# Reordering two start-up transposes on TensorE and moving satisfied waits of ScalarE to a later stage

## The chip, the cores and the metric

One core of one Trainium2 chip. The metric is device time in microseconds (us) of one execution. In the profile of the kernel before, that time is the span (first to last instruction) plus 1.2 to 1.3 us. "Granted clock" is the share of TensorE's full clock that the chip let it run at. All executions below count as undisturbed ones ("fast").

## The reference, cut to what matters

Two branches share the input x (2048 tokens of 640): linear attention with a softmax feature map, and a SwiGLU FFN of width 1728. A sigmoid gate, one number per token, mixes them.

```python
g = sigmoid((x * gate_w).sum(-1, keepdims=True))
a = attention(x, wqkv, w_phi, wo)      # phi(q) (phi(k)^T v) / (phi(q) . sum phi(k)), then @ wo
b = (silu(x @ w_gate) * (x @ w_up)) @ w_down
out = g * a + (1 - g) * b
```

## The kernel before

Every operation is one letter in a list that is worked through in order, and every engine gets its instructions in that order. `H` is a pair of dummy matmuls, `G` transposes the gate row, `X t` transposes token tile t, `U t.c` is part c (of five) of v tile t, `V` a whole v tile, `F b.k` an FFN item, `M` premultiplies K's weights by the feature map's, `K` a key tile, `a` 88 waits on ScalarE, `N` the end of the kv sums. The other letters don't matter here.

```python
ORDER = """
H0 H1 a H2 H3 H4 H5 H6 H7 H8 H12 G X0 H9 H10 U0.0 X1 H11 U1.0 U0.1 U1.1 X2 U2.0 U0.2 U1.2 U2.1
X3 U2.2 U0.3 U1.3 U2.3 U0.4 U1.4 U2.4 V3 Y F0.1 M1 i3 M0 F0.0 M2 V4 M3 M4 K0 K1 ...   # cut
"""
def act_waits():                                  # 'a'
    for _ in range(NWAIT):                        # 88
        act.wait_ge(tr.sem["pe"], 1)              # true since the first dummy pair
def xpose(t):                                     # 'X'
    pr = next_pair()
    for c0, c1 in (((0, 1), (1, 5)) if t < 3 else ((0, 5),)):
        o = bankbf(2 * pr + (c0 > 0), 640)
        transposes([(o[:, c * P:(c + 1) * P], xs[:, t, c * P:(c + 1) * P]) for c in range(c0, c1)])
        copy("dve", xT[:, t, c0:c1, :].rearrange("p c k -> p (c k)"), o[:, c0 * P:c1 * P])
def v_out(t, pr):                                 # after a v tile's last part
    ...                                           # cut
    copy("act", o, i)                             # the first ScalarE computation of the program
    copy("act", svec[:, t:t + 1], bank(2 * pr + 1, 320, 321))
def kv_end():                                     # 'N'
    for _ in range(NPEW):                         # 24
        pe.wait_ge(tr.sem["pe"], 1)
    ...                                           # cut
```

The softmax here doesn't subtract the row's maximum and nothing guards it: scores larger than these inputs give would overflow.

Of the kernel before, what the change touches and what calls it, by code (L numbers as in the profile page):

```python
# [15 lines left out]
NPE = 4  # L16
NV = 6
NWARM = 2
NWAIT = 88
NPEW = 24  # L20
FP = 120 * NCH
FK = FP + 8
ACTF = mybir.ActivationFunctionType
# [12 lines left out]
"""  # L36

ORDER = """
H0 H1 a H2 H3 H4 H5 H6 H7 H8 H12 G X0 H9 H10 U0.0 X1 H11 U1.0 U0.1 U1.1 X2 U2.0 U0.2 U1.2 U2.1
X3 U2.2 U0.3 U1.3 U2.3 U0.4 U1.4 U2.4 V3 Y F0.1 M1 i3 M0 F0.0 M2 V4 M3 M4 K0 K1 I S0 V6 V5 S1 P0  # L40
K3 K2 P1 E0 V9 K4 E1 S3 V7 P3 K5 S2 V8 V10 S4 P2 P4 E2 R0 E3 K6 S5 P5 S6 i4 E4 V14 K7 K8 P6 V15 S7
R2 E5 K9 S8 P7 R1 E6 K10 S9 V12 P8 E7 P9 K11 S10 P10 F0.2 R3 F1.2 E8 E9 K12 E10 S11 S12 K14 S14
# [11 lines left out]
class _Tracker:  # L54
# [90 lines left out]
    def run(self, eng, fn, reads=(), writes=(), dma=False):  # L145
        rkeys = list(dict.fromkeys(k for a in reads for k in self.keys_of(a)))
        wkeys = list(dict.fromkeys(k for a in writes for k in self.keys_of(a)))
        need = {}

        def req(ev, raw):  # L150
            if ev is None:
                return
            s, v = ev
            if s == eng and not dma and (eng == "pe" or not raw):
                return
            if v > need.get(s, 0):
                need[s] = v

        for k in rkeys:
            for kk in self._conflicts(k):  # L160
                req(self.lastw[kk], True)
                if k[0] == "psum":
                    for s, v in self.readers[kk].items():
                        req((s, v), False)
        for k in wkeys:
            for kk in self._conflicts(k):
                req(self.lastw[kk], True)
                for s, v in self.readers[kk].items():
                    req((s, v), False)
        self._wait(eng, need)  # L170
        ins = fn()
        if dma:
            sn = "d%d" % self.ndma
            self.ndma += 1
            self._add_sem(sn)
            inc = 16
        else:
            sn, inc = eng, 1
        ins.then_inc(self.sem[sn], inc)
        self.cnt[sn] += inc  # L180
        v = self.cnt[sn]
        snap = dict(self.known[eng])
        if not dma:
            snap[sn] = max(snap.get(sn, 0), v)
        self.evknow.setdefault(sn, {})[v] = snap
        ev = (sn, v)
        for k in wkeys:
            self.lastw[k] = ev
            self.readers[k] = {}
        for k in rkeys:  # L190
            r = self.readers[k]
            if r.get(sn, 0) < v:
                r[sn] = v
        return ev


def _build(nc, A_x, A_wqkv, A_w_phi, A_wo, B_x, B_w_gate, B_w_up, B_w_down, gate_w, out):
    tr = _Tracker(nc)
    pe, act, dve, pool, sp = nc.tensor, nc.scalar, nc.vector, nc.gpsimd, nc.sync
# [76 lines left out]
    def bank(b, c0, c1, r0=0, r1=P):  # L276
        return ps[r0:r1, b * 512 + c0:b * 512 + c1]
# [9 lines left out]
    def mm(pairs):  # L287
        reads, writes = [], []
        for p in pairs:
            reads += [p[1], p[2]]  # L290
            writes.append(p[0])

        def fn():
            last = None
            for o, l, r, st, sp_, sk in pairs:
                last = pe.matmul(o, lhsT=l, rhs=r, start=st, stop=sp_, skip_group_check=sk)  # L296
            return last
        return run("pe", fn, list({id(a): a for a in reads}.values()), writes)

    def group(o, lr):  # L300
        n = len(lr)
        return [(o, l, r, i == 0, i == n - 1, False) for i, (l, r) in enumerate(lr)]
# [9 lines left out]
    def actop(o, i, func, scale=1.0):  # L312
        rd = [i] + ([scale] if isinstance(scale, bass.AP) else [])
        return run("act", lambda: act.activation(o, i, func, scale=scale), rd, [o])  # L314
# [7 lines left out]
    def tt(e, o, a, b, op):  # L322
        eo = tr.eng[e]
        return run(e, lambda: eo.tensor_tensor(o, a, b, op), [a, b], [o])  # L324

    def stt(o, a, s, b, op0, op1):
        rd = [a, b] + ([s] if isinstance(s, bass.AP) else [])
        return run("dve", lambda: dve.scalar_tensor_tensor(  # L328
            out=o, in0=a, scalar=s, in1=b, op0=op0, op1=op1), rd, [o])
# [45 lines left out]
    def load_ffn(c0, c1):  # L375
        dma("sp", wg[:, :, c0:c1], B_w_gate[:, c0:c1].rearrange("(c p) j -> p c j", p=P))
        dma("sp", wu[:, :, c0:c1], B_w_up[:, c0:c1].rearrange("(c p) j -> p c j", p=P))
# [19 lines left out]
    H0 = [0, 6, 12, 19, 25]  # L397
    H1 = [7, 13, 20, 26, 32]
# [24 lines left out]
            memset("pool", ph[:, :, :], 0.0)  # L423
            memset("pool", zh[:, NCH:P], 0.0)

    def act_waits():
        for _ in range(NWAIT):
            act.wait_ge(tr.sem["pe"], 1)

    for i in range(3):  # L430
        fills(i)

# [21 lines left out]
    def next_pair():  # L454
        return used([r for r in ring["lru"] if r < ring["n"] and r not in held][0])
# [224 lines left out]
    def fitem(bt, k):  # L680
        buf = bt % 2
        pr = next_pair()
        xr = [xT[:, 4 * bt:4 * bt + 4, c, :] for c in range(5)]
        u = us[:, nus[0] % 3, :]
        nus[0] += 1
        if k < 13:
            g, up = bank(2 * pr, 0, 512), bank(2 * pr + 1, 0, 512)
            h = hT[:, buf, k, :]
            mm(group(g, [(wg[:, c, P * k:P * k + P], xr[c]) for c in range(5)]))
            mm(group(up, [(wu[:, c, P * k:P * k + P], xr[c]) for c in range(5)]))  # L690
        else:
            mm(group(bank(2 * pr, 0, 512), [(wt[:, c, :], xr[c]) for c in range(5)]))
            g, up = bank(2 * pr, 0, 512, 0, 64), bank(2 * pr, 0, 512, 64, P)
            h, u = hT[0:64, buf, k, :], u[0:64]
        actop(h, g, ACTF.Tanh, 0.5)
        actop(u, up, ACTF.Copy)
        stt(h, h, 1.0, g, ALU.add, ALU.mult)
        tt("pool", h, h, u, ALU.mult)
# [43 lines left out]
    def kv_end():  # L742
        for _ in range(NPEW):
            pe.wait_ge(tr.sem["pe"], 1)
        kv_finish()
        ring["n"] = 4
# [3 lines left out]
        "M": lambda m: premult(1, m), "R": lambda m: premult(0, m),  # L750
        "K": ktile, "S": knorm, "P": kmul, "p": lambda t: kmul(t, "dve"), "E": kvtile, "x": load_x, "t": load_xt, "w": load_wv, "h": load_phi, "k": lambda m: load_wt(1, m), "q": lambda m: load_wt(0, m),
        "f": lambda i: load_ffn(FCUT[i], FCUT[i + 1]), "L": load_late_weights, "T": tail_weights, "J": gates,
        "Y": w_blocks, "a": lambda: act_waits(), "I": kv_begin, "N": kv_end, "Z": z_row,
        "Q": qtile, "A": qsum, "B": qden, "C": qscale, "c": qmul,
        "F": fitem, "O": oitem, "D": ditem,
    }
    for w in LOADS.split() + ORDER.split():
# [4 lines left out]
def bass_gated_mix__linear_kernel_hedgehog__swiglu_ffn__prompt_kernel(  # L762
    nc: bass.Bass,
    A_x: bass.AP,
    A_wqkv: bass.AP,
    A_w_phi: bass.AP,
    A_wo: bass.AP,
    B_x: bass.AP,
    B_w_gate: bass.AP,
    B_w_up: bass.AP,  # L770
    B_w_down: bass.AP,
    gate_w: bass.AP,
    out: bass.AP,
):
    _build(nc, A_x, A_wqkv, A_w_phi, A_wo, B_x, B_w_gate, B_w_up, B_w_down, gate_w, out)
# [28 lines left out]
```

## Time and profile before

| | before, first profile | before, second profile |
|---|---|---|
| time of that execution, us | 289.45 | 289.25 |
| span, us | 288.2 | 288.0 |
| first matmul of the first FFN item, us | 12.10 | 11.89 |
| last matmul's start, us | 286.11 | 285.90 |
| from the one to the other, us | 274.02 | 274.02 |

The second profile was taken after the prediction. The median before was 290.37 us of 3 runs when the prediction was written, and 290.72 of 6 in the comparison that followed. The views that the argument rests on are in the prediction and are not shown again.

### The profile page before, as it was taken

How to read it: one execution, taken by the hardware profiler on the slowest of the kernel's cores; microseconds unless marked ns; L12 is line 12 of the kernel's file. 1: busy time of each engine (PE TensorE's matmuls, PEld its weight loads, DVE VectorE, ACT ScalarE, POOL GpSimd, SP SyncE). 2: the span in 40 equal slices, each digit the busy share in tenths (PEclk: the TensorE clock that was granted, in tenths of full speed). 3: DMA queues.
4: the chain of work that ended last, by engine and by line, in shares of the span. 5: the costliest groups of instructions: out<-in, count | busy, mean ns of one | idle time of the engine just before them, and what ended most of it. 6: DMA issues, size and time to landing. Idle time of an engine off the chain costs nothing.

```text
span 288.2 us, 4961 instructions
## 1 busy us (share of the span) xinstructions
PE 284.9 (99%) x1975; PEld 174.8 (61%) x1975; DVE 163.5 (57%) x243; ACT 151.6 (53%) x252; POOL 159.8 (55%) x125
## 2 busy tenths in 40 slices
PE   8999999999999999999999999999999999999997
PEld 6567777575644445557775556675554446656776
DVE  2146748577469978679991475970317899100000
ACT  0678768666685566583445753225676552234112
POOL 8286899879545789836633438350753558501000
PEclk9999999999999999999999999999999999999999
DMA  6975789000020498302292002061020006210101
GB/s 209 185 113 125 113 212 369 9 0 3 0 50 0 104 306 152 63 2 50 55 165 63 12 1 50 2 144 47 2 50 0 3 1 123 52 45 0 49 23 48
DMA packets 48944, 21.62 MB, mean 75 GB/s; under 512 B 39384, under 2 KB 48792, under 8 KB 48920
## 3 DMA queue, kind: packets, MB, share of 16 engines
q1 hardware_dynamic: 48190, 20.62, 31.5%
q10 hardware_dynamic: 730, 0.68, 0.7%
q8 instruction: 16, 0.26, 0.4%
q14 instruction: 8, 0.07, 0.1%
HBM read 9.29 MB, written 2.62 MB: 41 GB/s over the span
## 4 chain that ended last, share of the span: by engine, by line
PE 98%; ACT 1%; DVE 0%; issue 0%; ACTq 0%
PE ps L296 97%; PE ps L478 1%; PE ps L308 1%; ACT L314 0%; ACT v1r L314 0%; DVE xT L320 0%; DVE osb L730 0%; ACTq L139 0%; ACT svec L314 0%
## 5 line engine op out<-in xcount | busy, mean ns | idle before, releaser
L324 POOL TENSOR_TENSOR hT<-hT,us 128x512 bf16<-128x512 bf16 (+1 forms) x56 | 65.0, 1173 | 67.0 <-DVE hT L328 50.1
L328 DVE SCALAR_TENSOR_TENSOR hT<-hT,ps 128x512 bf16<-128x512 bf16 (+1 forms) x56 | 37.4, 683 | 69.0 <-ACT hT L314 55.3
L296 PE MATMUL ps<-xT,wg 128*128 128x512 bf16 x260 | 64.6, 379 | 0.4 <-ACT svec L314 0.4
L296 PE MATMUL ps<-xT,wu 128*128 128x512 bf16 x260 | 64.6, 379 | 0.0
L296 PE MATMUL ps<-wd,hT 128*128 128x320 bf16 (+2 forms) x462 | 63.9, 295 | 0.0
L324 POOL TENSOR_TENSOR ph<-eq,qc 128x1320 bf16<-128x1320 bf16 x16 | 42.3, 2645 | 25.6 <-DVE qc L638 20.8
L296 PEld LDWEIGHTS ps<-wd,hT 128*128 128x128 bf16 x462 | 44.5, 98 | 17.4
L296 PE MATMUL ps<-wqk,xT 128*128 128x320 bf16 x320 | 47.7, 299 | 0.0
L314 ACT ACTIVATE hT<-ps 128x512 bf16<-128x512 f32 (+2 forms) x60 | 35.8, 597 | 16.0 <-PE ps L296 15.8
L296 PEld LDWEIGHTS ps<-xT,wu 128*128 128x128 bf16 x260 | 25.5, 98 | 30.6
L314 ACT ACTIVATE us<-ps 128x512 bf16<-128x512 f32 (+1 forms) x56 | 33.5, 598 | 19.2 <-PE ps L296 18.2
L296 PEld LDWEIGHTS ps<-xT,wg 128*128 128x128 bf16 x260 | 25.0, 98 | 28.4 <-ACT oT L314 0.8
L314 ACT ACTIVATE osb<-ps,omg 128x640 bf16<-128x640 f32 (+2 forms) x17 | 12.9, 757 | 55.8 <-PE ps L296 55.8
L324 POOL TENSOR_TENSOR ekr<-ekr,krec 128x1280 bf16<-128x1280 bf16 x16 | 37.4, 2357 | 5.7 <-DVE krec L338 5.7
L296 PEld LDWEIGHTS ps<-wqk,xT 128*128 128x128 bf16 x320 | 30.5, 98 | 13.1 <-issue 0.4
L314 ACT ACTIVATE eq<-ps 128x640 bf16<-128x640 f32 x32 | 22.3, 703 | 20.8 <-POOL ph L324 10.6
L335 DVE TENSOR_REDUCE ksum<-ekr 128x64 f32<-128x1280 bf16 x16 | 23.5, 1471 | 11.7 <-ACT ekr L314 11.7
L314 ACT ACTIVATE ekr<-ps 128x640 bf16<-128x640 f32 x32 | 22.3, 703 | 8.7 <-PE ps L296 8.2
L335 DVE TENSOR_REDUCE qz<-eq 128x64 f32<-128x1280 bf16 x16 | 23.7, 1479 | 2.6 <-ACT eq L314 2.6
L296 PE MATMUL ps<-wvg,xT 128*128 128x320 bf16 (+1 forms) x160 | 24.6, 301 | 0.1
L296 PE MATMUL ps<-wog,oT 128*128 128x320 bf16 (+2 forms) x165 | 24.7, 295 | 0.0
L335 DVE TENSOR_REDUCE qw<-ez 128x64 f32<-128x1280 bf16 x16 | 23.6, 1477 | 0.0
(73 smaller groups left out, 189.8 us busy)
## 6 DMA issues: line engine op xcount, KB each, us to landing
out_dram<-osb SPq DMA_DIRECT2D x15, 160.0 KB, 1.9
wd<-in_B_w_down_dram SPq DMA_DIRECT2D x1, 2080.0 KB, 9.5
wg<-in_B_w_gate_dram SPq DMA_DIRECT2D x1, 1040.0 KB, 9.5
wu<-in_B_w_up_dram SPq DMA_DIRECT2D x1, 1040.0 KB, 10.7
wg<-in_B_w_gate_dram SPq DMA_DIRECT2D x1, 800.0 KB, 5.6
wu<-in_B_w_up_dram SPq DMA_DIRECT2D x1, 800.0 KB, 7.2
wog<-in_A_wo_dram SPq DMA_DIRECT2D x2, 375.0 KB, 7.2
wvg<-in_A_wqkv_dram SPq DMA_DIRECT2D x4, 160.0 KB, 4.0
```

The costliest lines, as they stand in the source:

```text
L296: last = pe.matmul(o, lhsT=l, rhs=r, start=st, stop=sp_, skip_group_check=sk)
L308: last = pe.transpose(o, i, ident[0:k, 0:k])
L314: return run("act", lambda: act.activation(o, i, func, scale=scale), rd, [o])
L324: return run(e, lambda: eo.tensor_tensor(o, a, b, op), [a, b], [o])
L328: return run("dve", lambda: dve.scalar_tensor_tensor(out=o, in0=a, scalar=s, in1=b, op0=op0, op1=op1), rd, [o])
L335: return run("dve", lambda: dve.tensor_reduce(o, i, AX.X, ALU.add), [i], [o])
L478: last = pe.matmul(bank(2 * pr, 0, P), lhsT=c, rhs=c, start=True, stop=True)
```

## The change

Its intent: TensorE's start-up is reordered so that copies hide behind other work, and the spare waits leave the start of ScalarE's stream, where they stood ahead of its first computation. They come back in the third FFN stage, and TensorE gets eight more waits at the end of the kv sums, so that the instruction streams stay nearly as long as they were. Two of the 26 dummy matmuls go.

```diff
-NWAIT = 88
-NPEW = 24
+NWAIT = 6
+NPEW = 32
-H0 H1 a H2 H3 H4 H5 H6 H7 H8 H12 G X0 H9 H10 U0.0 X1 H11 U1.0 U0.1 U1.1 X2 U2.0 U0.2 U1.2 U2.1
+H0 H1 H2 H3 H4 H5 H6 G H7 H8 X0 H9 H10 U0.0 X1 H11 U1.0 U0.1 X2 U1.1 U2.0 U0.2 U1.2 U2.1
-    def act_waits():
-        for _ in range(NWAIT):
-            act.wait_ge(tr.sem["pe"], 1)
@@ fitem
+        if bt == 2:
+            for _ in range(NWAIT):
+                act.wait_ge(tr.sem["pe"], 1)
         actop(h, g, ACTF.Tanh, 0.5)
```

More of the change, by code (lines that the diff above doesn't have):

```diff
@@ L752, in _build @@
         "f": lambda i: load_ffn(FCUT[i], FCUT[i + 1]), "L": load_late_weights, "T": tail_weights, "J": gates,
-        "Y": w_blocks, "a": lambda: act_waits(), "I": kv_begin, "N": kv_end, "Z": z_row,
+        "Y": w_blocks, "I": kv_begin, "N": kv_end, "Z": z_row,
         "Q": qtile, "A": qsum, "B": qden, "C": qscale, "c": qmul,
```

## The prediction

> **What bounds the kernel now.** I read the page's busy shares first, then the waits of TensorE, then the chain of work that ended last, then the timeline of the first 14 us.
>
> ```profile
> PE 284.9 (99%) x1975; PEld 174.8 (61%) x1975; DVE 163.5 (57%) x243; ACT 151.6 (53%) x252; POOL 159.8 (55%) x125
> ```
>
> TensorE is busy for 284.9 of 288.2 us and every other engine for under 60%. So the span is TensorE's work plus TensorE's holes, and a change that alters no matmul of the real work can only win or lose holes. The waits of TensorE, which list only the holes the profile calls idle, are two:
>
> ```profile
> PE ps L478 <- PEq L789: 0.8, 1, 0.8
> PE ps L296 <- ACT svec L314: 0.4, 1, 0.4
> ```
>
> The chain of work (start us, us, what) shows where the head of the kernel loses time and that nothing is lost later:
>
> ```profile
> 6.48 0.07 PE ps L308
> 6.55 0.02 issue
> 6.57 0.23 DVE xT L320
> 6.80 0.05 issue
> 6.85 1.27 PE ps L296 x8
> 8.12 0.28 PE ps L308 x5
> 8.40 1.39 PE ps L296 x10
> 9.79 0.02 issue
> 9.81 0.04 ACTq L139
> ...
> 9.95 1.28 ACT L314
> 11.24 0.01 issue
> 11.25 0.71 ACT v1r L314
> 11.95 0.07 ACT svec L314
> 12.02 0.07 issue
> 12.10 66.26 PE ps L296 x616
> 78.36 0.05 PE ps L308
> 78.41 207.92 PE ps L296 x1271
> ```
>
> From 12.10 us to 286.33 us it is matmul after matmul. A matmul's modelled end overlaps the next, so I also took the start-to-start steps of all 1975 matmul records against the usual step of their size (136 ns for 320 columns, 216 for 512, 55 for 128 once warm). After 12.1 us only eight steps are over by more than 25 ns, some 94 ns each, at the four tiles' kvsb matmuls. Before it: 0.25 us at 4.36 us (the first v part waits for weights landing at 4.22), 0.21 us at 6.85 us (x2's copy on VectorE, the 0.23 us above), and 0.56 us at 12.10 us, where the first FFN item waits until ScalarE has emptied the first v tile's banks. ScalarE is late because of this:
>
> ```profile
> 8.24 3.46 PE L296 MATMUL ps<-wvg,xT 128*128 128x320 bf16 x24
> 12.10 1.24 PE L296 MATMUL ps<-xT,wg 128*128 128x512 bf16 x5 [0.40 <-ACT svec L314]
> 9.95 1.28 ACT L314 ACT_TABLE_LOAD   x1 [9.95 <-PE ps L296]
> 11.25 0.71 ACT L314 ACTIVATE v1r<-ps 128x640 bf16<-128x640 f32 x1
> 11.85 0.17 ACT L314 ACTIVATE svec<-ps 128x1 f32<-128x1 f32 x1
> ```
>
> The table load starts only after the matmul that the first evacuation needs. In the built program waits are packed two to an instruction, and with 88 spare waits in front the real wait on TensorE (semaphore at 34) slides forward into a wait instruction ahead of the load. The spare waits themselves are done early: this view of their line gives 43 records, 3.2 to 6.4 us.
>
> ```profile
> L428 ACTq EVENT_SEMAPHORE  x43: 17/38/38, 3.2 to 6.4; - x43
> ```
>
> **What the Trainium skill says.** "ScalarE: Activation LUTs", section What ACT_TABLE_LOAD costs, gives about 1283 ns for the load itself; the trace has 1.28 us, and the new program has exactly one load too. "Perfetto Trace Analysis", section Identifying Dependency Chains, says that instructions waiting on several engines may get EventSemaphore instructions ahead of them; the 43 records for 88 waits agree. "TensorE: Matmul & The Clock Gate", Part 1, puts the rise of the clock around 4 us into activity, ±500 ns from run to run. Here matmuls of 128 columns step by 107 ns from 0.84 us and by 55 from about 5.2 us, 4.3 us in. "Runtime: NRT & Kernel Launch", section Instruction fetch mechanics, says instructions come in 16 KiB blocks; the page's instruction queue q8 has 16 packets and 0.26 MB, so TensorE's do, and its last such packet falls at 285.2 us, near the end.
>
> **The change part by part.**
>
> (1) Start-up dummies: 26 become 24, and the gate row's transpose comes after 14 instead of 20. x0 lands at 3.08 us whichever order is used, and the first v part waits for weights landing at 4.22 us. Before, x0 was transposed at 3.18. Four dummies after the gate row end near 0.84 + 18 x 0.107 + 0.11 + 0.14 = 3.0 us. The first v part stays at 4.36 us: 0.
>
> (2) x2 ahead of v part U1.1. Before: six matmuls (U1.0, U0.1, U1.1) from 5.48, x2 from 6.32, a hole, U2.0 at 6.85. After: x2 from 6.04 (landed 5.56; its second bank waits for x1's second copy, done at 5.93), its first column block finished by about 6.26, copied by 6.52, while U1.1's two matmuls fill 6.32 to 6.59. U2.0 starts at about 6.59 instead of 6.85: **0.26 us earlier**. The next limits: x3 lands at 7.56 and its matmul was at 7.96, w3 at 8.05 against 8.51. They leave 0.36 and 0.41 us after a floor of about 0.05, so the 0.26 passes.
>
> (3) No waits ahead of the table load. In the new program the load waits only for the memset of the v tiles (GpSimd, done by about 5 us), so it ends near 6.2 us; the wait for TensorE sits on the evacuation. That then runs at 9.79 - 0.26 = 9.53 us instead of 11.25 and is done near 10.3, before V3's last matmul. The **0.56 us** hole goes; its gate and up weights landed at 9.30 and 10.41. The FFN item starts at 12.10 - 0.26 - 0.56 = 11.28 us.
>
> (4) But loads do not come earlier. Setting each landing against the first matmul that waits for it, three early ones are close: premultiply M2's weights land at 16.33 for a matmul at 17.04 (0.71), M4's at 18.49 for 19.05 (0.56), the others have 1.3 us or more. A released matmul starts 0.05 us after its landing at best (x2's copy shows 0.046). So TensorE may shift 0.66 us at M2 and **0.51 us** at M4. Of the 0.26 + 0.56 = 0.82 us won, 0.31 is given back waiting for M2's and M4's weights. From there the K tiles follow M4 through the same copies, and all later stages shift together.
>
> (5) 84 waits in the third FFN stage: 6 per item, 14 items, three wait instructions each at a pace of 75 ns (two of them at 9.81 and 9.89), 0.23 us per item, 3.2 us of ScalarE. Most of them pass while ScalarE waits for TensorE anyway; the last of the three holds the real wait, so a tanh starts at most 0.1 us later after its matmul. In 154 to 222 us ScalarE is busy 36.6 of 68 us. The closest bank releases of that stage stand 0.51 us or more ahead of the matmul that needs them: 0.
>
> (6) Eight more waits on TensorE, four instructions at a pace of 0.106 us, 0.42 us. The eleven old ones run from 75.8 to 76.9 us while the queue still holds Q2's matmuls until 78.19. The margin falls from some 1.1 to 0.7 us: 0. Counted in the two programs, TensorE's instructions go from 4045 to 4046 and ScalarE's from 360 to 358: these added waits keep the streams' lengths, so the block that is fetched at the end stays where it was.
>
> Sum: 290.37 - 0.51 = **289.9 us**.
>
> **The rivals.** (a) Loads land earlier or M4's limit is not real: the full 0.82 us, 289.5. For: landings of that stage differ between executions, and the transposing loads are issued one after another on SyncE with steps from 1.26 to 3.8 us. Against: in this trace M4's slack is 0.56. (b) The head's gain is eaten wholly, because landings decide when the K stage starts, or because the clock rises half a microsecond later: 290.4. For: the skill's ±500 ns and a DMA share over 0.8 in the first 12 us. Against: no hole before M2 in the trace. (c) ScalarE's added waits turn into a TensorE hole in the third stage: from 198.6 to 204.8 us ScalarE works without a break, and three items of 0.23 us could add 0.7 us there, giving 290.6. Against: 0.5 to 0.9 us of slack, and only some of the items there are of that stage. (d) The end: a shift of the last instruction fetch against the last stores, a few tenths either way.
>
> **Range and chances.** The three timed runs before reach from 290.0 to 291.07, and the profiled one took 289.45, so the noise of a median of three (some 0.3 us) is as large as the gain. Rival (a) sets 289.5 and (c) 290.6; with the noise around them I take 289.2 to 290.8. Two per cent is 5.8 us, eleven times the gain; the whole of TensorE's holes before 12.1 us plus the end after 286.3 would not make it, and no part adds a serial cost near it. Same 0.97, faster 0.02, slower 0.01.
>
> **What would show it.** Right: the table load ends before 8 us, the wait of 0.4 us on svec is gone, U2.0 starts near 6.6 us, the FFN item near 11.3, and M2 or M4 starts within 0.1 us of its weights' landing; TensorE ends some 0.5 us earlier. (4) is wrong if the K stage starts 0.8 us earlier or not earlier at all. (5) and (6) are wrong if TensorE shows a new hole between 154 and 270 us, or near 78 us. The whole is wrong if the last matmul moves by more than 1 us.

## The result, and the profile after

The kernel after took 289.3 us in the median of 6 runs (288.35 to 289.61), the kernel before 290.72 us in the same rounds (290.0 to 291.73): ratio 0.9942, 95% interval 0.9915 to 0.997. Ratios here are the mean time of one kernel's fast runs over that of the other's of the same rounds, so not quite the ratio of the medians. By the medians the gain is 1.4 us, where the prediction had 0.5 (the 289.3 us lie at the low end of its range). Yet the profiled execution after has a span of 288.0 us, only 0.2 less than the first profile before. That contradiction is what the experiments had to settle.

The waits of TensorE in the kernel after: the one on svec is gone, and a load has come in its place.

```profile
PE ps L474 <- PEq L788: 0.8, 1, 0.8
PE ps L296 <- DMA wvg<-in_A_wqkv_dram: 0.7, 2, 0.4
```

ScalarE's timeline of the kernel after (start us, us, instruction): the table load starts at 5.01 us instead of 9.95 and is over long before the first evacuation, which begins at 10.20 instead of 11.25.

```profile
5.01 1.28 ACT L314 ACT_TABLE_LOAD   x1 [5.01 <-POOL v1r L342]
10.20 0.71 ACT L314 ACTIVATE v1r<-ps 128x640 bf16<-128x640 f32 x1 [3.91 <-PE ps L296]
```

The chain that ended last in the kernel after (start us, us, what) begins with a load. The second piece of the v weights landed at 6.37 us, against 5.38 in the first profile before. That ate most of what the closed holes had given: the first FFN item starts at 11.92 us, inside the long piece that begins at 8.79.

```profile
1.73 4.64 DMA wvg<-in_A_wqkv_dram
...
6.41 0.45 PE ps L296 x2
...
8.79 69.40 PE ps L296 x640
```

From the first matmul of the first FFN item to the last matmul of all, the kernel after takes 274.02 us, as before, to 10 ns. The same stretch was measured in all 20 traces: 274.01 or 274.02 us in 18 of them, whatever ScalarE's and TensorE's waits were, and 274.30 and 274.31 in two that come up below. **So, those two apart, everything that the change did to the span lies before that matmul**, in the head of the kernel, and the question is what that head does from one execution to the next.

### The profile page after: what moved, and what is told of

Read it like the earlier page.

```text
span 288.0 us, 4960 instructions
## 1 busy us (share of the span) xinstructions
PE 284.6 (99%) x1973; PEld 174.1 (60%) x1973; DVE 163.5 (57%) x243; ACT 151.8 (53%) x252; POOL 159.8 (55%) x125
## 4 chain that ended last, share of the span: by engine, by line
PE 97%; DMA 2%; SPq 0%; DVE 0%; issue 0%
PE ps L296 97%; DMA wvg<-in_A_wqkv_dram 2%; SPq L350 0%; PE ps L308 0%; DVE osb L729 0%
## 6 DMA issues: line engine op xcount, KB each, us to landing
wu<-in_B_w_up_dram SPq DMA_DIRECT2D x1, 1040.0 KB, 11.9
```

## The experiments

All are single-core kernels with correct results. Each call brought its own runs of the kernel before on the same chip. "F" is the start of the first FFN item's first matmul.

| kernel | runs | mean us | before, mean us (runs) | ratio, 95% interval |
|---|---|---|---|---|
| again_before | 6 | 290.11 | 290.38 (11) | 0.9993 (0.9957 to 1.0029) |
| again_after | 6 | 289.58 | same | 0.9969 (0.9937 to 1.0001) |
| act_only | 6 | 290.07 | same | 0.9986 (0.9954 to 1.0018) |
| pe_only | 6 | 290.65 | same | 1.0006 (0.997 to 1.0041) |
| third_after | 6 | 289.75 | 290.01 (11) | 0.9988 (0.995 to 1.0026) |
| no_pad | 6 | 290.48 | same | 1.0009 (0.9973 to 1.0045) |
| filled | 6 | 289.16 | same | 0.9968 (0.9939 to 0.9997) |
| w0_first | 6 | 291.51 | same | 1.0049 (1.0015 to 1.0083) |
| filled_before | 5 | 289.88 | 289.70 (11) | 1.0005 (0.9991 to 1.0019) |
| filled_again | 6 | 289.39 | same | 0.9988 (0.9973 to 1.0003) |
| no_act_pad | 6 | 289.51 | same | 0.9992 (0.9972 to 1.0012) |
| no_pe_pad | 6 | 289.59 | same | 0.9996 (0.9972 to 1.0019) |
| after_share_1, _2 | 12 | 289.60 | 289.97 (11) | 0.9985 (0.9954 to 1.0017), 0.9996 (0.9972 to 1.002) |

### The two kernels again, and each half of the change alone

> The kernel before, unchanged, for a second profile and as a control of the comparison. Both theories: ratio 1.000 within 0.003. Theory 'head': everything after the first FFN item's first matmul takes 274.0 us as in the two traces at hand (12.10 to 286.11 before, 11.92 to 285.94 after), so this profile differs from the first one only in when that matmul starts; the timed runs (290.0 to 291.7) put a usual start near 13.0 to 13.5 us, not 12.1, because loads land later or the clock rises later than in the first profile. Rival 'later stages': the stretch after the first FFN item is longer than 274.0 us in a usual execution of this kernel.

> The kernel after, unchanged, for a second profile. Theory 'head': 0.994 (0.991 to 0.997) as before, 274.0 us after the first FFN matmul, its start between 11.0 and 12.2 us. Rival 'later stages': the stretch after is under 274.0 us in some executions.

`act_only` is the kernel after with the old order and `NPEW = 24`; `pe_only` is the kernel before with the new order and `NPEW = 32`:

```diff
 act_only, against the kernel after:  NPEW = 24, and
+H0 H1 H2 H3 H4 H5 H6 H7 H8 H12 G X0 H9 H10 U0.0 X1 H11 U1.0 U0.1 U1.1 X2 U2.0 ...
 pe_only, against the kernel before:  NPEW = 32, and
+H0 H1 a H2 H3 H4 H5 H6 G H7 H8 X0 H9 H10 U0.0 X1 H11 U1.0 U0.1 X2 U1.1 U2.0 ...
```

> Only ScalarE's part of the change: no waits ahead of the table load, 6 per item in the third FFN stage; TensorE's order and its 24 waits as before. Theory 'head': the table load starts near 5.0 us, the wait of TensorE on svec is gone, gain 0.4 to 0.9 us, ratio 0.997 to 0.9985; x2's hole of 0.2 us stays. Rival 'the order of the transposes makes the gain': ratio 0.999 or more.

> Only TensorE's part: gate row amid the dummies, x2 ahead of U1.1, 32 waits; the 88 waits on ScalarE stay at the start, so the table load stays behind the first v tile's last matmul. Theory 'head': x2's hole closes, the wait on svec stays near 0.5 us, gain 0.1 to 0.4 us, ratio 0.9985 to 0.9997. Rival 'the order makes the gain': ratio near 0.994 to 0.996.

Measured: the stretch after F is 274.0 us in all four, so "later stages" falls. F itself is 11.89 us in again_before and 13.23 us in again_after: the kernel *after* gave the later head this time. The times cannot tell the halves apart (both intervals hold 1.000), the traces can. act_only has its table load at 5.03 us and no wait on svec; pe_only keeps that wait of 0.4 us (the step to F is 0.56 us too long). A miss: the guess that the kernel before usually has F at 13.0 to 13.5 us was wrong too; its second profile has 11.89. And the 13.23 us lie outside the 11.0 to 12.2 expected for again_after.

The slow heads have a cause in the trace. This is TensorE's timeline in again_after (start us, us, matmuls, what the idle time before waited for):

```profile
5.26 0.69 PE L296 MATMUL ps<-wvg,xT 128*128 128x320 bf16 x2 [1.00 <-DMA wvg<-in_A_wqkv_dram]
5.74 0.74 PE L308 MATMUL ps<-ident,xs 128*128 128x128 bf16 x5
...
7.56 0.74 PE L308 MATMUL ps<-ident,xs 128*128 128x128 bf16 x5
8.09 1.72 PE L296 MATMUL ps<-wvg,xT 128*128 128x320 bf16 x10
9.65 0.44 PE L308 MATMUL ps<-ident,xs 128*128 128x128 bf16 x5
```

The same five transposes take 0.74 us at 5.74 and 7.56 us and 0.44 us at 9.65: the clock rose at 8.5 us here, against 5.2 in the first profile before and 5.0 in the profile after. The first piece of the v weights landed at 5.12 us instead of 4.2 to 4.4 and left a hole of 1.0 us behind the dummies. In act_only and pe_only it landed at 5.00, and the clock rose near 9.8 and 9.0 us. So two things scatter in the head, **when a load lands and when the clock rises**, and together they moved F by over 2 us.

The clock records in the traces show how it moves between its two states. In after_share_1 (below) it changed at 4.02, 7.43 and 10.85 us, in primed_before at 5.49, 12.31 and 15.73 us: each change is one or two steps of 3.41 us after the one before, and where these steps lie against the first dummy (at 0.84 us in all traces) differs from execution to execution. So part of the scatter needs no late load. In no_pe_pad (below) the first piece landed at 4.20 us, the profile counts no gap of TensorE over 0.1 us, and the clock still rose only at 7.1 us. Late pieces go with late clocks all the same: in the five traces where that piece landed at 4.68 us or later the clock rose at 7.2 to 9.8 us, in the other six unprimed ones with these loads and dummies (no_pe_pad apart) by 5.3 us.

### The head primed, so that loads and clock cannot touch it

```diff
 def warm(i):                       # 'H'
-            for _ in range(NWARM):
+            for _ in range(100 if i == 0 else NWARM):
 def xpose(t):
+        if t == 0:
+            pe.wait_ge(tr.sem["d11"], 16)      # the up weights' first piece, near 10.4 us
```

> The kernel before with 98 more dummy matmuls at the start and x0's transpose held until the gate and up weights' first piece has landed (near 10.4 us), so that neither a late load nor a late rise of the clock can touch the head: 6 to 7 us longer than the kernel before. Theory 'the spread of the times is the head's loads and clock': timed runs within 0.6 us of each other (2.8 us for the kernel before). It is the base of the three that follow: x2's hole of 0.2 us and the wait on svec of 0.4 us (0.56 us beyond the usual step) must both be in its trace. Rival 'the spread is elsewhere': it stays at 2 us or more.

> The kernel after, primed in the same way. Theory 'two holes, 0.26 + 0.56 us': 0.8 us less than primed_before (0.7 to 0.95), from the start of the first v part to the first FFN item in the trace 0.8 us less, and 274.0 us after it. Rival 'the order and waits do more than the two holes': 1.0 us or more. Rival 'M4's weights cap the gain at 0.5 also here': 0.5; not expected, as the premultiplies come 6 us later than the loads.

> act_only, primed in the same way. Theory 'two holes': 0.56 us less than primed_before (0.45 to 0.65). Rival: near 0 or over 0.8.

> pe_only, primed in the same way. Theory 'two holes': 0.2 to 0.3 us less than primed_before, the wait on svec as long as there. Rival: 0.5 us or more.

The priming worked only in part. The wait for that landing leaves a hole of 1 to 2 us in front of x0, and in 5 of 25 runs the clock fell again (mean granted clock 0.994 instead of 1.000, near 298 us). The landing itself scattered (10.9 to 11.9 us in the traces), so the times did not shrink to within 0.6 us. Over all runs the means are 296.58 (before, 7 runs), 295.70 (act, 6), 296.39 (pe, 6) and 296.55 us (after, 6), so these times by themselves show no gain of the kernel after: three of its six runs met the fallen clock. Without those five runs the means are 296.24 (before, 6 runs), 295.70 (act, 6), 296.02 (pe, 5) and 295.17 us (after, 3): 0.54, 0.21 and 1.06 us less, with standard errors of 0.2, 0.3 and 0.4 us. The traces tell more, one of each kernel, since the stretch from the first v part to F is free of waits for loads here. The lines below are the first v part, the last v stretch and the first FFN matmul of primed_pe:

```profile
12.15 0.45 PE L296 MATMUL ps<-wvg,xT 128*128 128x320 bf16 x2
15.46 3.46 PE L296 MATMUL ps<-wvg,xT 128*128 128x320 bf16 x24
19.32 1.02 PE L296 MATMUL ps<-xT,wg 128*128 128x512 bf16 x4 [0.40 <-ACT svec L314]
```

and these the same of primed_after:

```profile
11.89 0.45 PE L296 MATMUL ps<-wvg,xT 128*128 128x320 bf16 x2
15.20 3.46 PE L296 MATMUL ps<-wvg,xT 128*128 128x320 bf16 x24
18.50 0.81 PE L296 MATMUL ps<-xT,wg 128*128 128x512 bf16 x3
```

19.32 - 12.15 = 7.17 us against 18.50 - 11.89 = 6.61: ScalarE's part is worth **0.56 us**. The first v part and the first FFN matmul of primed_act:

```profile
11.46 0.45 PE L296 MATMUL ps<-wvg,xT 128*128 128x320 bf16 x2
18.34 1.02 PE L296 MATMUL ps<-xT,wg 128*128 128x512 bf16 x4
```

It takes 18.34 - 11.46 = 6.88 us, so the order is worth 6.88 - 6.61 = **0.27 us**. These are the predicted sizes (0.56 and 0.26). The trace of primed_before caught a fallen clock and can't be set beside them; again_before, which met no late load after its first v part, has 11.89 - 4.46 = 7.43 us, what 6.61 + 0.56 + 0.27 makes.

### Third run of the kernel after: M4's weights

> The kernel after once more, as the base of the three that follow on the same chip. Holes theory: 0.5 to 1.2 us less than the kernel before; if its trace is one with early loads, M4's premultiply starts within 0.2 us of the landing of its weights; 274.0 us from the first FFN matmul to the last one.

Its trace shows the give-back that the prediction's part (4) expected. This is the weight loads' timeline around M3 and M4:

```profile
18.54 0.42 PEld L296 LDWEIGHTS ps<-wbd,wT 128*128 128x128 bf16 x6
19.26 0.31 PEld L296 LDWEIGHTS ps<-wbd,wT 128*128 128x128 bf16 x6 [0.30 <-DMA wT<-in_A_wqkv_dram]
```

M4 waits 0.30 us for weights that landed at 19.22 us (M4's matmul starts 0.05 us after), and the stretch after F is 274.31 us instead of 274.02: all of that wait goes into the end.

### Without the added waits

> The kernel after without its 84 waits on ScalarE and its 32 on TensorE. Theory 'they cost nothing and win nothing on the chip': the same as third_after within its noise (0.5 us), 274.0 us after the first FFN matmul to within 0.05 us, and the end after the last matmul as long (2.1 us). Rival 'they keep the last instruction fetch out of the end': the stretch after the last matmul, or the time beyond the span (1.27 us), grows by 0.3 us or more. Rival 'the spread waits delay ScalarE': the stretch after the first FFN matmul shrinks.

```diff
-NWAIT = 6
-NPEW = 32
+NWAIT = 0
+NPEW = 0
```

They cost nothing: the stretch after F is 274.02 us with and without them. They win something, which the span doesn't show. The time beyond the span is 1.5 to 2.8 us in the six runs of no_pad, mean 2.13, against 1.19 to 1.28 in third_after. What the transfer view of no_pad shows for 286 to 292 us, with its span ending at 288.5 (queue, kind: packets, MB, share), and the same view of third_after does not:

```profile
q8 instruction: 1, 0.02, 1.1%
q14 instruction: 1, 0.01, 0.4%
```

The q14 packet starts at 289.7 us and the q8 packet at 290.3: instructions are still being fetched after the work is done. In the kernels before and after, the last such packets come near 285 us on q8 and 268 on q14. Two more runs split the waits:

> The kernel after without the 84 waits on ScalarE, with the 32 on TensorE. In no_pad the time beyond the span was 1.5 to 2.8 us instead of 1.2 to 1.3, and its trace has the last instruction packets at 289.7 (small packets) and 290.3 us (16 KB), after the span's end at 288.5. If ScalarE's stream is the one behind the small packet at 289.7: 1.5 us or more beyond the span here. If TensorE's alone matters: 1.2 to 1.3 us, and the same time as the kernel after.

> The kernel after without the 32 waits on TensorE, with the 84 on ScalarE. If TensorE's stream is the one behind the 16 KB packet at 290.3 us: 1.5 us or more beyond the span here, that packet after the end. If ScalarE's alone matters: 1.2 to 1.3 us. 274.0 us from the first FFN matmul to the last in both.

Neither stream is the culprit alone. Beyond the span no_act_pad has 1.29 to 1.45 us and no_pe_pad 1.22 to 1.42, some 0.1 us more than usual, though the small packet comes after the end (290.7 us, span 289.4) in no_act_pad as well. In no_pe_pad none comes after it, but its profile has 15 packets on q8 where all others have 16, so one may lie outside what it caught. Why it takes both to lose some 0.9 us stays open.

### Filling the hole before the first v part

```diff
 def warm(i):
-            for _ in range(NWARM):
+            for _ in range(10 if i == 10 else NWARM):   # 8 more dummies behind X0
```

> The kernel after with 8 more dummy matmuls behind x0's transpose, which keep TensorE working until 4.9 us. Theory 'a late first piece of the v weights (5.0 instead of 4.3 us) leaves a hole of 1 us in the warm-up, and the clock then rises one window later': the clock rises before 7.7 us in its trace whenever that piece lands, and the slow end of the times (over 290 us) goes, at up to 0.5 us in the quick executions: 288.8 to 290.0 in all. Rival 'the rise is chance': times over 290.2 as often as with third_after, a rise after 8 us possible.

> The kernel before with the same 8 more dummies behind x0's transpose as in filled. Theory 'the change wins its two holes, 0.8 us, less what M4's weights take back': 0.5 to 0.9 us slower than filled_again, and no runs over 291 us, as the late clock needs the hole that the dummies fill. Rival 'the change wins 1.4 us': 1.2 us or more slower. Both holes are in its trace, F to the last matmul 274.0 us.

> The kernel filled once more, on the chip of filled_before: 288.6 to 289.8 us, 0.995 to 0.998 of the kernel before. Rival 'the first result was a lucky draw': over 290.2 us in two or more of the six.

filled is the kernel after with this edit, filled_before the kernel before with it. All 17 runs lie between 288.71 and 290.08 us, and the clock rises before 5.7 us in the three traces. None was slow, while third_after beside the first of them had 290.64 and 291.54. That fits the hole as a cause of the late clock but does not prove it: the first v weights landed early in all three traces (3.80 to 4.12 us), and on the chip of the last two the kernel before had no slow run either.

What the pair is for: filled_before 289.88 us, filled_again 289.39 us. **With the slow end out of both, the change is worth 0.49 us, standard error 0.16.** filled_before has its wait on svec; filled_again has M4 as the thing that limits it, in the chain that ended last:

```profile
14.87 3.48 DMA wT<-in_A_wqkv_dram
18.35 0.05 issue
18.39 59.32 PE ps L296 x562
```

It has F at 11.17 us, near the predicted 11.28, and then M4 starts 0.05 us after the landing at 18.35 and TensorE has idled 0.28 us for it (the stretch after F is 274.30). 0.83 - 0.28 = 0.55.

filled is also the best version found: 0.9968 and 0.9988 of the kernel before. Its mean of 289.28 us (12 runs) against 289.54 of the kernel after (30 runs) is not a proven gain, since they come mostly from other chips; its runs scatter less (standard deviation 0.34 against 0.84 us).

### The first v weights earlier

```diff
-x0 w0 x1 w1 ...        WQ = ["sp", "sp", "sp", "sp", "act"]
+x0 w0 g x1 w1 ...      WQ = ["act", "sp", "sp", "sp", "act"]     # g: the gate row's load, after w0
+... H8 G X0 ...
```

> The kernel after with the first piece of the v weights issued first on ScalarE's queue, the gate row behind it, and the gate row's transpose just ahead of x0's. Theory 'the head waits for that piece and the clock follows': the piece lands by 3.8 us, the first v part starts near 4.1 instead of 4.4 to 5.3 us, no hole of over 0.4 us before it, the clock rises before 7.7 us, 0.3 to 1.0 us less than third_after on average. Rival 'the later pieces or M4's weights (near 18.5 us) set the head': within 0.3 us of third_after, with M4 waiting for its weights.

A failed attempt. The piece did land early (3.82 us), but x0 landed at 3.64 instead of 3.0, the gate row at 3.79 instead of 2.2, and x1 at 6.13 instead of 4.5: 1.8 us slower than third_after, with 0.9 us of TensorE waiting for the gate row and 0.5 for x1, and a clock that rose at 8.5 us, again behind holes.

### How often the head is slow

> The kernel after, for the share of slow executions. Slow means the head's part of the clock or loads is late: over 290.5 us here (291 us less the 0.5 us won) against over 291 us for the kernel before. Theory 'the draw': the share is that of the kernel before on the same chip (about a quarter), and the quick runs are 0.4 to 0.8 us under its quick runs. Rival 'the change makes slow executions rarer': none or one of the twelve, with three or more of the eleven before.

> As after_share_1, the second six of the twelve runs, read together with it: a share of slow ones near the kernel before's, or none or one.

Two of twelve runs after are over 290.5 us (291.81, 290.75), none of the eleven before is over 291. Over all runs, 15 of 67 before are over 291 us and 5 of 30 after over 290.5. So nothing shows that the change makes slow heads rarer, and in the recorded comparison three of six before were slow and none of six after. The limits are my choice, though the 67 times do leave a gap between 290.67 and 291.07. The remaining, quick runs have means of 289.82 (52 runs) and 289.23 us (25): 0.59 us. All runs: 290.21 and 289.54: 0.67 us, standard error 0.18. Chips are mixed in these sums. By call the difference is -1.67 (the recorded comparison), -0.70, -0.27 and -0.36 us. Without the recorded comparison it is 290.15 (61 runs) against 289.63 us (24), 0.51 us with a standard error of 0.21, and 0.54 us (0.12) for the quick runs.

The trace of after_share_1 caught a slow head of a second kind. The clock had risen at 4.0 us; then the second piece of the v weights landed at 7.23 us, TensorE idled 1.5 us for it, and the clock fell. By stages (us, busy time and count of PE, PEld, DVE, ACT, POOL, then the granted clock, DMA share, GB/s):

```profile
4.10:7.40 3.30, 1.51 (x14) 0.82 (x13) 0.89 (x3) 1.28 (x1) 2.99 (x5) 1.00 0.93 274
7.40:10.80 3.40, 3.40 (x17) 2.15 (x16) 0.65 (x2) 0.00 (x0) 0.00 (x0) 0.50 1.35 238
10.80:14.20 3.40, 3.40 (x30) 2.45 (x28) 1.27 (x3) 1.48 (x5) 1.44 (x3) 0.99 0.60 120
```

At half clock TensorE is as busy as ever in the second row and does 17 matmuls where the third row has 30. F is 14.45 us here, the latest of all unprimed traces.

## Why the prediction was right or wrong, point by point

- **What bounds the kernel: right.** No stretch after F changed in any trace except by a wait for M4's weights.
- **(2) and (3), the two holes: right in mechanism and size.** 0.27 and 0.56 us in the primed traces, against 0.26 and 0.56 predicted. The table load moved to 5.01 us, and F reached 11.17 us with quick loads.
- **(4), the give-back at M4: right, and variable.** 0.29 and 0.28 us in the two traces whose loads made it bind, none in the others; 0.31 was predicted. M4's weights landed between 17.31 and 19.44 us over the traces.
- **(5) and (6), the added waits: free, as predicted.** That they keep the streams' lengths was a reading of counts; without both, 0.9 us appear beyond the span.
- **The failed step is the base of the sum (290.37 us) with its noise, and the 0 of part (1) behind it.** The prediction took one trace's landings and clock as every execution's ("The first v part stays at 4.36 us: 0") and put the noise of a median of three at "some 0.3 us". The runs showed a head that is drawn anew each time: the first v part started at 4.3 to 5.3 us in the traces of the unprimed kernels with the original loads, the clock rose at 4.0 to 9.8 us, and the times of the kernel before have a standard deviation of 0.82 us over 67 runs, with a group of slow heads over 291 us; medians of 11 runs of it on different chips ran from 289.62 to 291.21. The term for the change itself, 0.51 us, measured 0.49 us in the filled pair and 0.51 us over the runs outside the recorded comparison.
- **Where the recorded 1.4 us come from is shown in part.** By means that comparison has 1.67 us. Three slow heads of the kernel before against none of the kernel after make about 0.6 of it. But its three quick runs before (mean 290.21 us) and six runs after (289.15) still differ by 1.06 us, standard error 0.23, against 0.54 us in the later calls, and its 95% interval, some 0.9 to 2.5 us, does not contain 0.5. A draw of few runs on both sides is the likeliest reason; that the change is worth more on that chip was not tested. That 289.3 us lies inside the predicted range is owed to the width of the range, not to the sum.
- **Rivals.** (b) named the right quantity, the late clock, but as something that would eat the gain, and at half a microsecond; it scatters from 4.0 to 9.8 us over the traces and strikes both kernels. (a) holds in executions where M4 doesn't bind. (c) did not happen. (d) did not happen in the kernel after (1.2 to 1.3 us beyond the span, as before); with both streams shortened something like it did.

What stays open: how much of the late clock the late first piece causes (they came together in five traces, but no run forced that load late, and no_pe_pad has a clock at 7.1 us without it), why the first loads land as they do, and the rest of the recorded difference.

## What to carry to other kernels

Split a time into the part that repeats and the part that doesn't before sizing a change of half a microsecond: here 274.02 of 288 us repeat to 10 ns in 18 of 20 traces, and nearly all the noise sits in the first 12 to 14 us of loads and clock. A comparison of such a change needs the noisy part controlled (here by dummies that bridge the late load), or tens of runs. And look at where a table load stands: waits packed ahead of the first activation can put a real wait in front of it, so that its 1.28 us come after that wait; here TensorE lost 0.56 us by it.

## What the Trainium skill lacked or had wrong

- "TensorE: Matmul & The Clock Gate", section Why this matters for your kernels: it asks for no idle gaps over about 3 us between bursts. Here a gap of 1.5 us (after_share_1) and one of 1.8 us (primed_before) were each followed by 3.4 us at half clock, while a gap of 2.0 us in primed_pe was not.
- The same page, Part 1: it puts the rise around 4 us into sustained activity, ±500 ns. From the first dummy at 0.84 us it took 3.2 us (after_share_1) to 6.2 us (no_pe_pad, with no gap over 0.1 us), and 9.0 us in act_only, behind a hole of 0.8 us.
- "Runtime: NRT & Kernel Launch", section Instruction fetch mechanics: it gives 16 KiB blocks for the refill and calls the cost mostly hidden. Queue q8 has 16 KB packets here, but q14 has 8 packets in 0.07 MB, half as large, and with both streams shorter the time beyond the span grew from 1.2 to 2.1 us on average.
- "ScalarE: Activation LUTs", section What ACT_TABLE_LOAD costs: besides 1283 ns it counts a drain of about 1380 ns for every switch to a different set, and does not set a first load apart. The first load here took 1.28 us and the activation behind it began 0.01 us later: no drain.
- No page that I found gives the scatter of a first load: the same 160 KB piece of the v weights, issued second on its queue, landed between 3.80 and 5.12 us.
